# Fifteen small unread loads on ScalarE's DMA queue, in a decode-attention and SwiGLU kernel

## The chip, the cores and the metric

The kernel runs on one core of a Trainium2 chip. The metric is the time of one execution in microseconds (us), as the device measures it. A kernel's time is the median of its runs. "The profile" is one execution taken by the hardware profiler; its span is somewhat shorter than the measured time (136.8 us in the profile of the kernel before, against 138.75 us). "The trace" is what that profile was made from: each instruction, each semaphore update and each DMA packet with its start and length.

## The reference, cut to what matters

```python
h  = x + A(layernorm(x))      # A: q = x @ wq; attention over the last 2048 keys of k_cache and v_cache; @ wo
h2 = h + B(layernorm(h))      # B: (silu(h @ w1) * (h @ w3)) @ w2
# x is 4 x 1024, wq 1024 x 4096, k and v windows 4 x 4 x 2048 x 128, wo 4096 x 1024,
# w1 and w3 1024 x 3584, w2 3584 x 1024, all bf16
```

Four rows of x meet some 55 MB of weights and cache, so nearly all the work is loading.

## The kernel before: the parts that matter

All large loads go out on SyncE's queue, in one fixed order, into five buffers of 4 MB. x is loaded on ScalarE's queue.

```python
def load_rows(src, n, r0, pieces):
    t = stream.tile([P, SLOT], BF16, tag="s")              # 5 buffers
    i = 0
    for m in pieces:
        nc.sync.dma_start(
            out=t[:, i * n : (i + m) * n], in_=src[:, (r0 + i) * n : (r0 + i + m) * n]
        )
        i += m
    ...

# plan: wq in three loads (2 MB, 2 MB, 4 MB), k in four of 2 MB, v in four, wo, w1, w3, w2
x_sb = act.tile([B, D], BF16)
nc.scalar.dma_start(out=x_sb[:], in_=x_flat)
load_next(5)                                               # wq, k and half of v, as buffers allow
...
for j in range(JG):                                        # JG = 4
    nc.scalar.dma_start(
        out=x_q[QD * j : QD * (j + 1) : RS, :], in_=x_flat[:, j * CG : (j + 1) * CG]
    )
...
nc.scalar.activation(out=rstd[:], in_=mv[:, 1:2], func=ACT.Sqrt, ...)   # ScalarE's first activation
... # xn = layernorm(x), transposed; then the query matmuls q_ps, one group for each wq load
```

A completion semaphore is a counter that a DMA raises as it lands; whoever needs its data waits for the count. No semaphore is written in the source. The tile framework adds them when the program is built. In the built programs, the DMAs of SyncE's and ScalarE's queues together use **eight completion semaphores**, dealt out in turn in the order in which the framework schedules the DMAs. A DMA that is dealt a semaphore with an earlier holder is given a wait, on its issuing engine, for that holder's landing. This is the start of the deal before (numbers are semaphores 0 to 7):

```
x_sb 0, wq1 1, x_q 2 3 4 5, wq2 6, wq3 7          none of these waits for a holder
k1 waits for 0 (x_sb), k2 for 1 (wq1), k3 and k4 for 2 and 3 (x_q), v1 and v2 for 4 and 5, v3 for 6 (wq2), ...
```

## Time and profile before

| | before |
|---|---|
| time, median of 2 runs | 138.75 us (138.73 to 138.77) |
| span of the profile | 136.8 us |
| moved by DMA | 55.74 MB, mean 407 GB/s |
| busy: matrix engine, VectorE, ScalarE | 50%, 31%, 22% of the span |

From the page of the kernel before, the span in 40 equal slices of 3.42 us: the busy share of the 16 DMA engines in tenths, and what they moved.

```profile
DMA  5999999999999999999999999999999999998950
GB/s 156 441 418 503 402 393 441 421 431 436 421 431 421 436 436 417 433 445 469 450 421 402 407 427 441 453 441 402 427 449 453 411 419 424 450 460 364 418 219 2
```

The DMA engines never rest between the first slice and the last three. In the views below, L95 is line 95 of the kernel, PE is the matrix engine, DVE is VectorE and ACT is ScalarE; SPq and ACTq are instructions that issue DMAs on SyncE's and ScalarE's queues, and "issue" is time in which nothing was waited for. The chain of work that ended last (start, length, what) ends so:

```profile
95.26 0.42 SPq L95
95.69 0.04 issue
95.73 37.38 DMA t<-in_B_w_dram
133.11 0.04 issue
133.15 0.32 PE y_ps L430 x4
133.49 0.42 DVE res L440
```

The last load is issued at 95.7 us and lands 37.4 us later, because that much is queued ahead of it. The waits of the matrix engine for loads (total us, times, longest us):

```profile
PE q_ps L213 <- DMA t<-in_A_wq_dram: 11.9, 3, 7.8
PE u_ps L400 <- DMA t<-in_B_w_dram: 10.9, 2, 5.5
PE y_ps L430 <- DMA t<-in_B_w_dram: 8.1, 4, 6.5
PE g_ps L400 <- DMA t<-in_B_w_dram: 4.6, 1, 4.6
```

It waits at each stage of wq, w1, w3 and w2, so computing has slack there and the load stream has none. How the stream starts is in the timeline of SyncE's queue (start, length from the first to the last of the group, what):

```profile
0.73 1.47 SPq L95 DMA_DIRECT2D t<-in_A_wq_dram  x3
2.42 7.62 SPq L107 DMA_DIRECT2D t<-in_A_k_cache_dram  x4
```

and of ScalarE:

```profile
1.35 2.52 ACTq L146 DMA_DIRECT2D x_q<-in_A_x_dram  x4
3.90 1.28 ACT L160 ACT_TABLE_LOAD   x1 [3.90 <-DVE stats L156]
5.20 0.29 ACT L160 ACTIVATE rstd<-mv,eps_t 4x1 f32<-4x1 f32 x1
```

All three wq loads, 8.4 MB, are in the queue by 2.2 us.

### The profile page before, as it was taken

The page shows a single profiled execution, that of the slowest core. Times are in us where ns is not written, and L with a number is a line of the kernel's source. Part 1 is how long each engine was busy: PE and PEld are TensorE (multiplying, and loading weights), DVE is VectorE, ACT ScalarE, POOL GpSimd, SP SyncE. Part 2 cuts the span into 40 slices and gives each one's busy share as a digit, 9 for nine tenths or more (in the row PEclk, how much of TensorE's full clock was granted, in tenths as well). Part 3 has the DMA queues.
Part 4 walks back from the last instruction along what each step waited for, and adds up shares of the span by engine and source line. Part 5 has one row for each costly group of instructions (what it writes and reads, how often), then busy time and mean ns, then how long its engine had stood idle before and what let it go on. Part 6 is the DMA issues. An engine that isn't in the chain of part 4 may idle for free.

```text
span 136.8 us, 2307 instructions
## 1 busy us (share of the span) xinstructions
PE 68.3 (50%) x1035; PEld 42.3 (31%) x1035; DVE 43.0 (31%) x74; ACT 30.6 (22%) x35; POOL 1.7 (1%) x8
## 2 busy tenths in 40 slices
PE   0152303698989899105259259825080530802950
PEld 0110001274756565000149247602030210301820
DVE  6440000244444444709940030260004970170001
ACT  0400000155555646092943000000015000000000
POOL 5000000000000000000000000000000000000000
PEclk9999999999999999965555865896555586555586
DMA  5999999999999999999999999999999999998950
GB/s 156 441 418 503 402 393 441 421 431 436 421 431 421 436 436 417 433 445 469 450 421 402 407 427 441 453 441 402 427 449 453 411 419 424 450 460 364 418 219 2
DMA packets 3237, 55.74 MB, mean 407 GB/s; under 512 B 376, under 2 KB 408, under 8 KB 668
## 3 DMA queue, kind: packets, MB, share of 16 engines
q1 hardware_dynamic: 3188, 55.58, 95.2%
q8 instruction: 8, 0.13, 0.3%
q10 hardware_dynamic: 40, 0.02, 0.1%
q14 instruction: 1, 0.01, 0.0%
HBM read 55.59 MB, written 0.01 MB: 406 GB/s over the span
## 4 chain that ended last, share of the span: by engine, by line
DMA 43%; PE 29%; ACT 13%; DVE 8%; issue 4%; SPq 1%; ACTq 0%; DVEq 0%
DMA t<-in_B_w_dram 27%; DMA t<-in_A_wq_dram 15%; PE kt_ps L261 9%; ACT kT L267 6%; PE scores_ps L246 5%; PE OT_ps L324 5%; PE y_ps L351 4%; ACT z L302 3%; PE q_ps L213 2%; DVE rmax L278 2%; PE g_ps L400 2%; ACT Pm L283 2%; SPq L95 1%; DVE pT L292 1%; DVE z L298 1%
## 5 line engine op out<-in xcount | busy, mean ns | idle before, releaser
L267 ACT COPY kT<-kt_ps 128x1024 bf16<-128x1024 bf16 x16 | 15.8, 1014 | 12.0 <-PE kt_ps L261 12.0
L261 PE MATMUL kt_ps<-ident,t 128*128 128x128 bf16 x256 | 16.5, 220 | 0.0
L261 PEld LDWEIGHTS <-t 128*128 128x128 bf16 x256 | 14.4, 98 | 5.0 <-issue 4.9
L265 DVE COPY kT<-kt_ps 128x1024 bf16<-128x1024 bf16 x16 | 11.1, 692 | 15.2 <-PE kt_ps L261 15.2
L213 PE MATMUL q_ps<-t,xnT 128*4 128x512 bf16 x64 | 6.9, 596 | 11.9 <-DMA t<-in_A_wq_dram 11.9
L400 PEld LDWEIGHTS <-hnT 128*32 128x32 bf16 x128 | 4.9, 129 | 23.7 <-issue 20.8
L400 PE MATMUL u_ps<-t,hnT 128*32 128x448 bf16 x64 | 6.3, 573 | 10.9 <-DMA t<-in_B_w_dram 10.9
L246 PE MATMUL scores_ps<-kT,qz 128*32 128x512 bf16 x64 | 9.9, 609 | 3.1 <-ACT kT L267 2.9
L324 PE MATMUL OT_ps<-z,t 128*128 128x32 bf16 x256 | 7.5, 186 | 7.7 <-ACT z L302 5.0
L430 PE MATMUL y_ps<-t,hgT 128*32 128x256 bf16 x112 | 6.0, 384 | 8.1 <-DMA t<-in_B_w_dram 8.1
L324 PEld LDWEIGHTS <-t 128*128 128x128 bf16 x256 | 7.3, 102 | 8.4 <-issue 8.3
L400 PE MATMUL g_ps<-t,hnT 128*32 128x448 bf16 x64 | 5.2, 490 | 6.9 <-DMA t<-in_B_w_dram 4.6
L430 PEld LDWEIGHTS <-hgT 128*32 128x32 bf16 x112 | 4.6, 134 | 10.1 <-issue 5.8
L213 PEld LDWEIGHTS <-xnT 128*4 128x4 bf16 x64 | 2.0, 112 | 16.4 <-issue 16.0
L351 PE MATMUL y_ps<-t,o 128*32 128x256 bf16 x128 | 5.9, 372 | 0.8 <-DVE o L340 0.8
L223 DVE TENSOR_SCALAR q_sb<-q_ps 128x512 bf16<-128x512 f32 x1 | 0.7, 692 | 17.4 <-PE q_ps L213 17.4
L302 ACT ACTIVATE z<-pt_ps,mask 128x512 bf16<-128x512 f32 x8 | 5.3, 687 | 3.5 <-DVE z L298 3.5
L298 DVE TENSOR_SCALAR z<-pt_ps,mask 128x512 bf16<-128x512 f32 x8 | 5.5, 741 | 1.1 <-ACT z L302 0.8
L294 PE MATMUL pt_ps<-pT,perm 128*128 128x512 bf16 x4 | 2.4, 609 | 6.8 <-DVE pT L292 6.8
L414 DVE RECIPROCAL eg<-eg 128x896 f32<-128x896 f32 x1 | 5.8, 5752 | 0.0
L351 PEld LDWEIGHTS <-o 128*32 128x32 bf16 x128 | 4.4, 133 | 3.1 <-DVE o L340 1.9
L224 ACT ACTIVATE q_sb<-q_ps 128x512 bf16<-128x512 f32 x1 | 0.6, 597 | 21.1 <-DVE q_sb L223 21.1
(73 smaller groups left out, 40.3 us busy)
## 6 DMA issues: line engine op xcount, KB each, us to landing
t<-in_B_w_dram SPq DMA_DIRECT2D x4, 3584.0 KB
t<-in_A_k_cache_dram SPq DMA_DIRECT2D x4, 2048.0 KB, 25.4
t<-in_A_v_cache_dram SPq DMA_DIRECT2D x4, 2048.0 KB, 41.5
t<-in_A_wo_dram SPq DMA_DIRECT2D x2, 4096.0 KB, 42.2
t<-in_A_wq_dram SPq DMA_DIRECT2D x2, 2048.0 KB, 9.6
t<-in_A_wq_dram SPq DMA_DIRECT2D x1, 4096.0 KB, 21.0
t<-in_B_w_dram SPq DMA_DIRECT2D x1, 4096.0 KB, 37.7
t<-in_B_w_dram SPq DMA_DIRECT2D x1, 1280.0 KB, 34.4
```

The lines of the kernel that those rows point to most:

```text
L213: nc.tensor.matmul(q_ps[QD * g : QD * g + B, hf * 512 : (hf + 1) * 512], lhsT=xnT[:, kc, :], rhs=wq_t[:, c0 : c0 + 512], start=(kc == 0), ...
L246: nc.tensor.matmul(scores_ps[QD * g : QD * (g + 1), n * 512 : (n + 1) * 512], lhsT=qz[:, b, g * QD : (g + 1) * QD], rhs=kT_v[:, g, :, :], ...
L261: nc.tensor.transpose(out=kt_ps[:, jj, :], in_=k_v[:, n * NJ + t * TB + jj, :], identity=ident[:])
L265: nc.vector.tensor_copy(out=kT[:, t * TB : (t + 1) * TB, :], in_=kt_ps[:])
L267: nc.scalar.copy(out=kT[:, t * TB : (t + 1) * TB, :], in_=kt_ps[:])
L298: nc.vector.tensor_scalar(out=z[:, :, g, :], in0=pt_ps[:], scalar1=mask[:, g : g + 1], scalar2=None, op0=ALU.mult)
L302: nc.scalar.mul(out=z[:, :, g, :], in_=pt_ps[:], mul=mask[:, g : g + 1])
L324: nc.tensor.matmul(OT_ps[:, b, :], lhsT=loaded["v"][b][:, j, :], rhs=PTz[j // NJ][:, (j % NJ) * B + b, :, :], start=(j == 0), stop=(j == J ...
L351: nc.tensor.matmul(y_ps[QD * j : QD * (j + 1), :], lhsT=o4[:, i, :, :].rearrange("p b s -> p (b s)"), rhs=loaded["wo"][i][:, j * CG : (j + ...
L400: nc.tensor.matmul(out_ps[QD * j : QD * (j + 1), hf, :HF], lhsT=hnT[:, k, :], rhs=loaded[kind][k][:, c0 : c0 + HF], start=(k == 0), stop=( ...
L414: nc.vector.reciprocal(out=eg[:], in_=eg[:])
L430: nc.tensor.matmul(y2_ps[QD * j : QD * (j + 1), :], lhsT=hgT[:, i, :], rhs=loaded["w2"][i][:, j * CG : (j + 1) * CG], start=False, stop=(i ...
```

## The change

Fifteen small loads ("marks") of 1 to 15 rows of wq, each with its own row size of 32 to 256 bytes, follow the loads of x on ScalarE's queue. Nothing reads them, so the change can only show what such loads cost beside a full stream.

```diff
             out=x_q[QD * j : QD * (j + 1) : RS, :], in_=x_flat[:, j * CG : (j + 1) * CG]
         )
+
+    marks = wide.tile([16, 15, 128], BF16, tag="w4k")
+    for k in range(1, 16):
+        n = 8 + 8 * k
+        nc.scalar.dma_start(out=marks[0:k, k - 1, :n], in_=A_wq[0:k, 0:n])
```

The framework schedules eight marks ahead of the second wq load and the other seven ahead of the third. The deal in the built program of the changed kernel:

```
x_sb 0, wq1 1, x_q 2 3 4 5, marks 1 to 8: 6 7 0 1 2 3 4 5
wq2 6: waits for mark 1
marks 9 to 15: 7 0 1 2 3 4 5
wq3 6: waits for wq2
```

## The prediction

> What bounds the kernel now. It is bound by its stream of loads. The profile's slices show the DMA engines at 9 tenths in all but the first and the last few, at a mean of 407 GB/s. The chain of waits ends with 37.4 us of waiting for w2's last load, and the waits view shows the matrix engine idle for weights in every late stage (4.6, 5.5, 5.35 and 6.5 us). So computing has slack there, and the load stream has none: each microsecond in which SyncE's queue is empty should lengthen the run by about one.
>
> What the change adds. Under 20 KB. The x_q loads, of the same kind, take 0.63 us each to issue on ScalarE's queue (4 in 2.52 us, timeline), so 15 cost about 9.5 us of ScalarE before its first activation (now at 5.2 us). By itself that would hide: the query matmuls' last input lands at 22.6 us.
>
> What it moves is worse. The built programs show eight completion semaphores dealt out in turn to the DMAs of both queues; a DMA that gets a used one first waits for its former holder. Before, the three wq loads go out without a wait at 0.73 to 2.2 us. After, the second wq load waits for the first mark, and the third, which draws the same semaphore, waits for the second wq load's landing.
>
> First pause. The first mark stands in ScalarE's rings behind the four x_q loads. The Trainium skill, "DMA: Bandwidth & Descriptors", section "Queues, rings and completion order", says that each DMA engine takes turns between rings packet by packet. The trace agrees: x_q loads issued from 1.35 us move their first packets at 5.55 us only, and then a data and a completion packet each alternate with 0.61 us packets of wq. So the first mark cannot land before the first wq load has drained, at 7.2 to 7.7 us. I expect it at about 8.0. From issue to first packet the first wq load took 1.0 us, and its first packets 1.1 to 1.5 us against 0.61. Estimate: 2.2 us lost.
>
> Second pause. The second wq load would land at about 15 us (12.6 before); then landing, issue, first packet and ramp again. Estimate: 2.0 us lost. The third wq load lands at about 26.8 us instead of 22.6.
>
> ScalarE: marks 4 and 11 to 15 wait for the first wq load and for earlier marks; ScalarE is free at about 17 us, the query matmuls start at about 21 and the first half is done by 25, still before the third wq load. The k and v loads wait for marks too, but these land with over 10 us of loads still queued.
>
> Predicted: 138.75 + 4.2 = 143.0 us, range 141.4 to 145.2. Chances: faster by over 2% 0.01, within 2% 0.12, slower by over 2% 0.87.
>
> What would show it. The timeline of SyncE: second wq issue at about 8 us, third at about 15. Slices: GB/s low twice in the first 18 us, then as before. First activation at 17 to 19 us. The waits view: the last wait for wq ends at 26 to 27.5 us; w-stage waits unchanged.
>
> What would make it wrong. If the marks land while the first wq load still flows, the first pause shrinks. If marks on few rings land much later than estimated, k loads (which wait for marks 9 to 12) could open a third pause. If the later stream has hidden slack, less than 4 us shows.

## The result, and the profile after

| | before | after |
|---|---|---|
| time, median | 138.75 us (2 runs) | 144.3 us (143.84 and 144.75) |
| ratio, 95% interval | | 1.0398 (1.0362 to 1.0434): slower |
| span of the profile | 136.8 us | 142.9 us |
| moved by DMA | 55.74 MB | 55.77 MB |

The slices of the page after, 3.57 us each:

```profile
DMA  5939679999999999999999999999999999998950
GB/s 158 432 75 436 203 339 422 436 431 427 427 440 427 427 427 427 436 422 472 443 431 406 431 416 460 417 430 441 425 425 430 425 441 458 431 431 369 417 219 2
```

There are two holes, in the third slice and in the fifth and sixth. From the seventh on the rates are those of before. The timeline of SyncE's queue after, in short windows so that the three wq loads are not merged:

```profile
0.73 0.38 SPq L95 DMA_DIRECT2D t<-in_A_wq_dram  x1
8.66 0.33 SPq L95 DMA_DIRECT2D t<-in_A_wq_dram  x1
16.20 0.33 SPq L95 DMA_DIRECT2D t<-in_A_wq_dram  x1
16.57 2.73 SPq L107 DMA_DIRECT2D t<-in_A_k_cache_dram  x4
```

What SyncE's queue waited for (two lines that have no counterpart before):

```profile
SPq L95 <- DMA marks<-in_A_wq_dram: 7.5, 1, 7.5
SPq L95 <- DMA t<-in_A_wq_dram: 7.2, 1, 7.2
```

ScalarE, and the matrix engine's waits for loads:

```profile
3.90 12.46 ACTq L153 DMA_DIRECT2D marks<-in_A_wq_dram  x15
16.39 1.28 ACT L165 ACT_TABLE_LOAD   x1 [16.39 <-DMA marks<-in_A_wq_dram]
17.68 0.29 ACT L165 ACTIVATE rstd<-mv,eps_t 4x1 f32<-4x1 f32 x1
```

```profile
PE u_ps L405 <- DMA t<-in_B_w_dram: 10.7, 2, 5.4
PE y_ps L435 <- DMA t<-in_B_w_dram: 8.8, 4, 6.5
PE q_ps L218 <- DMA t<-in_A_wq_dram: 5.4, 1, 5.4
PE g_ps L405 <- DMA t<-in_B_w_dram: 4.2, 1, 4.2
```

The second wq load went out at 8.66 us, after 7.5 us of waiting for a mark, and the third at 16.20 us, after 7.2 us of waiting for the second. The waits for w1, w3 and w2 hardly changed.

The trace's DMA packets size the holes. No packet of SyncE's queue with data was moving on any engine for 2.06 us from 7.57 us and for 1.65 us from 15.52 us; before there is no such stretch of over 0.15 us. The completion packets of the second wq load begin at 12.03 us before and 15.05 after (3.0 us later), those of the third at 21.72 and 27.44 (5.7 us later), and the last 4 KB packets of the stream (those of the last load but one) end at 132.12 and 137.96 (5.8 us later). So the loss is made by 28 us and carried unchanged to the end. The packets also add up: from 4 to 32 us, averaged over the 16 engines, SyncE's queue moves no data for 4.7 us (3.7 us of it in the two full stops), and its large packets take 1.0 us longer than the usual 0.61 us per 16 KB and 1.21 us per 32 KB. Before, both sums are zero within 0.03 us. The profile is of the slower of the two runs, 144.75 us.

### The profile page after: what moved, and what is told of

Its sections match the earlier page's. It is cut to its first block, busy times and chain, and to the rows that moved or that the text cites. A ratio compares the mean times of both kernels' runs of the same rounds, so it can differ in the third digit from the quotient of the medians.

```text
span 142.9 us, 2324 instructions
## 1 busy us (share of the span) xinstructions
PE 69.5 (49%) x1035; PEld 43.1 (30%) x1035; DVE 43.0 (30%) x74; ACT 30.7 (21%) x35; POOL 1.7 (1%) x8
## 2 busy tenths in 40 slices
DMA packets 3478, 55.77 MB, mean 390 GB/s; under 512 B 616, under 2 KB 648, under 8 KB 908
## 4 chain that ended last, share of the span: by engine, by line
DMA 43%; PE 30%; ACT 11%; DVE 8%; issue 3%; ACTq 2%; SPq 1%; DVEq 0%
DMA t<-in_B_w_dram 26%; DMA t<-in_A_wq_dram 14%; PE kt_ps L266 10%; ACT kT L272 5%; PE scores_ps L251 5%; PE OT_ps L329 4%; PE y_ps L356 4%; DMA marks<-in_A_wq_dram 3%; ACT z L307 3%; PE q_ps L218 3%; PE g_ps L405 2%; ACTq L146 2%; DVE rmax L283 2%; ACT Pm L288 1%; DVE pT L297 1%
## 5 line engine op out<-in xcount | busy, mean ns | idle before, releaser
L266 PE MATMUL kt_ps<-ident,t 128*128 128x128 bf16 x256 | 17.5, 227 | 0.0
L266 PEld LDWEIGHTS <-t 128*128 128x128 bf16 x256 | 15.5, 102 | 4.9 <-issue 4.9
L405 PE MATMUL u_ps<-t,hnT 128*32 128x448 bf16 x64 | 6.3, 574 | 10.7 <-DMA t<-in_B_w_dram 10.7
L175 PE MATMUL tp_ps<-ident,xn 4*128 4x4 bf16 x8 | 0.7, 199 | 18.8 <-DVE xn L168 18.8
L329 PEld LDWEIGHTS <-t 128*128 128x128 bf16 x256 | 7.3, 103 | 7.4 <-issue 7.3
L405 PE MATMUL g_ps<-t,hnT 128*32 128x448 bf16 x64 | 6.3, 573 | 6.5 <-DMA t<-in_B_w_dram 4.2
L435 PEld LDWEIGHTS <-hgT 128*32 128x32 bf16 x112 | 4.3, 127 | 10.7 <-issue 6.4
L175 PEld LDWEIGHTS <-xn 4*128 4x128 bf16 x8 | 0.6, 163 | 18.8 <-DVE xn L168 18.8
L356 PE MATMUL y_ps<-t,o 128*32 128x256 bf16 x128 | 5.1, 329 | 0.8 <-DVE o L345 0.8
```

The costliest lines, as they stand in the source:

```text
L266: nc.tensor.transpose(out=kt_ps[:, jj, :], in_=k_v[:, n * NJ + t * TB + jj, :], identity=ident[:])
L329: nc.tensor.matmul(OT_ps[:, b, :], lhsT=loaded["v"][b][:, j, :], rhs=PTz[j // NJ][:, (j % NJ) * B + b, :, :], start=(j == 0), stop=(j == J ...
L356: nc.tensor.matmul(y_ps[QD * j : QD * (j + 1), :], lhsT=o4[:, i, :, :].rearrange("p b s -> p (b s)"), rhs=loaded["wo"][i][:, j * CG : (j + ...
L405: nc.tensor.matmul(out_ps[QD * j : QD * (j + 1), hf, :HF], lhsT=hnT[:, k, :], rhs=loaded[kind][k][:, c0 : c0 + HF], start=(k == 0), stop=( ...
L435: nc.tensor.matmul(y2_ps[QD * j : QD * (j + 1), :], lhsT=hgT[:, i, :], rhs=loaded["w2"][i][:, j * CG : (j + 1) * CG], start=False, stop=(i ...
```

## The experiments

Three theories:

- **A**: the marks take semaphores in the common deal, so that a wq load has to wait for a holder that lands late. The stream runs empty, and being the bound it hands the loss to the total.
- **B**: the marks hold up ScalarE (first activation at 17.68 instead of 5.20 us), and with it the query matmuls.
- **C**: many small packets slow the DMA engines themselves.

Twelve kernels ran, all correct, each in 3 rounds beside the kernel before, in three groups of four with one chip for each group (the kernel before took 138.83, 138.70 and 138.73 us there). "Loss" is a kernel's median less that of the kernel before in its group. "Idle" is the time within the stream in which no large data packet of SyncE's queue moves on any engine, and "end shift" how much later than 132.12 us the last 4 KB packet ends; both are from one profile each.

| kernel | time, us | ratio (95%) | loss | idle | end shift |
|---|---|---|---|---|---|
| n2, two marks | 138.64 | 0.9985 (0.997 to 1.0) | -0.2 | none | 0.0 |
| n3, three marks | 141.06 | 1.0159 (1.0141 to 1.0177) | 2.2 | 1.34 | 2.5 |
| n8, eight marks | 141.49 | 1.0197 (1.0176 to 1.0219) | 2.7 | 1.54 | 2.7 |
| chain, no marks, two waits | 143.52 | 1.0338 (1.0317 to 1.0359) | 4.7 | 1.38 + 1.27 | 5.2 |
| chain2, no marks, second wait | 141.19 | 1.0185 (1.017 to 1.02) | 2.5 | 1.27 | 2.4 |
| actbusy, no marks, ScalarE held | 138.62 | 0.9991 (0.9975 to 1.0008) | -0.1 | none | 0.1 |
| wqfirst, fifteen behind wq | 143.42 | 1.0338 (1.0322 to 1.0353) | 4.7 | 3.24 | 4.7 |
| sp, fifteen on SyncE's queue | 145.99 | 1.053 (1.0514 to 1.0545) | 7.3 | 4.91 | 7.1 |
| merged, one load | 138.89 | 1.0012 (0.9997 to 1.0026) | 0.2 | none | 0.1 |
| pool, fifteen on GpSimd's queue | 141.07 | 1.0166 (1.0148 to 1.0184) | 2.4 | none | 2.1 |
| pool1load, one load there | 138.81 | 1.0013 (0.9996 to 1.003) | 0.1 | none | 0.0 |
| pool1row, fifteen of one row there | 140.21 | 1.0112 (1.0097 to 1.0128) | 1.5 | none | 1.6 |

### How many marks: n2, n3, n8

```diff
-    for k in range(1, 16):
+    for k in range(1, 3):        # n2;  range(1, 4) in n3,  range(1, 9) in n8
```

The number of marks decides which semaphores the wq loads are dealt:

```
n2: wq2 waits for x_sb,   wq3 for wq1 (while wq2 still flows)
n3: wq2 waits for wq1,    wq3 for the first x_q load
n8: wq2 waits for mark 1, wq3 for mark 2 (which lands with it)
```

> Only the first two of the fifteen marks. Built program: the second wq load then waits for x_sb (landed at 2.5 us), the third wq load for the first wq load (landed at 8.2 us before), while the second wq load still has about 4 us to flow. Theory A (a load that waits for a semaphore's former holder empties the stream): no pause, 138.6 to 139.2 us. Theory B (each mark costs ScalarE issue time that delays the query matmuls): 2/15 of 5.5 us, so about 139.5 us. Theory C (small packets slow the DMA engines): also in proportion, under 139.5 us.

> One mark more than n2. Built program: now the second wq load waits for the landing of the first, and the third for an x_q load, so that it can follow at once. Theory A: exactly one pause, a step of 2.5 to 3.1 us over n2, 141.2 to 142.0 us, second wq issue at 8.2 us, third right behind it. Theories B and C: a step of about 0.4 us, 139.1 to 139.9 us.

> Eight marks. Built program: the second wq load waits for the first mark as in the changed kernel, but the third waits for the second mark, which lands with it. Theory A: one pause of about 3 us, 141.5 to 142.3 us, close to n3 although there are five more marks. Theories B and C: eight fifteenths of the loss, 141.7 us for 5.5 us, and clearly over n3 (by about 1.8 us). The pair n3 and n8 tells them apart.

SyncE's queue in n2, then in n3:

```profile
0.73 2.00 SPq L95 DMA_DIRECT2D t<-in_A_wq_dram  x2
8.21 0.33 SPq L95 DMA_DIRECT2D t<-in_A_wq_dram  x1
```

```profile
0.73 0.38 SPq L95 DMA_DIRECT2D t<-in_A_wq_dram  x1
8.04 0.81 SPq L95 DMA_DIRECT2D t<-in_A_wq_dram  x2
```

The third mark, three rows of 64 bytes, costs 2.4 us (141.06 less 138.64), and the next five cost 0.4 us together. In n2 a wq load also waits, until 8.21 us, but another 2 MB is in the queue meanwhile, and the wait is free. In n3 the queue is empty when the wait ends. That is the step of theory A; B and C, which go in proportion to the marks, fall as the cause of this step. It was a little under the 2.5 us expected, so that n3 came 0.1 us below its range, and n8 (141.49) missed its own by 0.01. Of the 0.4 us between n3 and n8, 0.3 go with the later end of the wait: the second wq load goes out at 8.32 us in n8 and 8.04 in n3.

### The waits without the marks: chain, chain2

```diff
+            d = nc.sync.dma_start(...)
+            if src is wq_v:
+                chain.append(d.ins)
+                if len(chain) > 1:                  # chain2: > 2
+                    tc.add_manual_dep(chain[-1], chain[-2].name, <wait for landing>)
```

> The kernel before, without any mark, but the second wq load made to wait for the landing of the first and the third for the landing of the second. Theory A: both pauses come without a mark, 143.6 to 144.6 us, second wq issue at 8.2 us, third at about 15.7. Theories B and C: no mark, no loss, 138.8 us.

> No marks; only the third wq load waits for the landing of the second, the second goes out at once. The second pause alone. From the runs so far (chain 143.5 less n3 141.1): 2.4 us, 140.9 to 141.4 us; third wq issue at 12.9 us, first k load landing 2.4 us later than before.

SyncE's queue in chain:

```profile
0.73 0.39 SPq L97 DMA_DIRECT2D t<-in_A_wq_dram  x1
8.19 0.33 SPq L97 DMA_DIRECT2D t<-in_A_wq_dram  x1
15.26 0.33 SPq L97 DMA_DIRECT2D t<-in_A_wq_dram  x1
```

With no mark in the program, the two waits alone cost 4.7 us of the 5.55. The waits are sufficient. The two add: the first pause alone costs 2.2 us (n3), the second alone 2.5 (chain2), and both together 4.7 (chain). chain came 0.1 us below its range. What remains to the changed kernel, about 0.9 us, goes with its longer holes: 2.06 + 1.65 us against 1.38 + 1.27. It is as large as the spread of the changed kernel's two runs, and so only roughly known.

### ScalarE held without marks: actbusy

```diff
+    junk = wide.tile([P, 2048], BF16, tag="w4k")
+    nc.gpsimd.memset(junk[:], 0.0)
+    junk2 = wide.tile([P, 2048], BF16, tag="w4k")
+    busy = [nc.scalar.copy(out=junk2[:], in_=junk[:]).ins for _ in range(6)]
-    nc.scalar.activation(out=rstd[:], in_=mv[:, 1:2], func=ACT.Sqrt, ...)
+    with tc.issue_after(busy[-1]):
+        nc.scalar.activation(out=rstd[:], in_=mv[:, 1:2], func=ACT.Sqrt, ...)
```

> No marks; six dummy copies of 128 x 2048 on ScalarE ahead of its first useful activation, which then comes at about 17 to 19 us, as in the changed kernel (17.7), instead of 5.2. Theory A: the query matmuls start late but the loads do not, 138.6 to 139.3 us. Theory B (ScalarE's delay is the cause): 143 us or more.

ScalarE in actbusy:

```profile
5.22 11.54 ACT L157 COPY junk<-junk 128x2048 bf16<-128x2048 bf16 x6
16.78 1.28 ACT L166 ACT_TABLE_LOAD   x1
18.07 0.29 ACT L166 ACTIVATE rstd<-mv,eps_t 4x1 f32<-4x1 f32 x1
```

The first activation is even later than in the changed kernel (18.07 against 17.68 us), and nothing is lost. Theory B falls.

### The pause moved: wqfirst, sp

In wqfirst the marks get an ordering edge, without a wait, to the third wq load, so that they are dealt their semaphores after it. In sp they are issued on SyncE's own queue, where the framework puts them after the first half of v.

```diff
 wqfirst:
-        nc.scalar.dma_start(out=marks[0:k, k - 1, :n], in_=A_wq[0:k, 0:n])
+        d = nc.scalar.dma_start(out=marks[0:k, k - 1, :n], in_=A_wq[0:k, 0:n])
+        tc.add_manual_dep(d.ins, chain[-1].name, <order only>)   # chain: the wq loads
 sp:
-        nc.scalar.dma_start(out=marks[0:k, k - 1, :n], in_=A_wq[0:k, 0:n])
+        nc.sync.dma_start(out=marks[0:k, k - 1, :n], in_=A_wq[0:k, 0:n])
```

> All fifteen marks on ScalarE's queue, but told to come behind the third wq load in the order in which the semaphores are dealt out. The wq loads then wait for nothing, but the first k load waits for the eighth mark, and that for the landing of the third wq load. Theory A: both early pauses are gone and one new one stands behind the third wq load, at about 22 to 25 us: one pause, 141.2 to 142.4 us; first wq inputs as before (22.6 us). Theories B and C: B 138.8 us (the first activation comes before the marks), C 144 us.

> All fifteen marks on SyncE's own queue, between the load of v's second part and its third. The wq and k loads wait for nothing new. Built program: the eighth mark waits for the landing of the second v load, which is the last load in the queue, and marks nine to fifteen are issued behind it before the next load of v. Theory A: one pause of about 4.4 us at 52 to 57 us (landing, eight issues of 0.3 us, first packet 1 us, slow first packets), 142.3 to 144.0 us, with all wq and k landings as before. Theories B and C: B 138.8 us (ScalarE is untouched); C a loss in proportion to the packets, which the deep queue should not change.

The chain of work in wqfirst, from its longest early wait on:

```profile
1.63 21.09 DMA t<-in_A_wq_dram
22.73 0.02 issue
22.75 1.28 DMA marks<-in_A_wq_dram
24.02 0.02 issue
24.04 7.93 DMA t<-in_A_k_cache_dram
```

The pauses at 7 and 15 us are gone and one stands where the deal says: mark 8 waits for wq3, and the first k load for mark 8. I had costed it as one pause of the usual size and missed the range (143.42 against 141.2 to 142.4): two landings stand in series, the second of 1.28 us, and the stream is idle for 3.24 us instead of 1.3 to 2.1. In sp the pause is far from the start. Busy time by stretch (start:end, length, then PE, weight loads, DVE, ACT and POOL, which is GpSimd, and PE's granted clock; the last two figures of a line are the DMA engines' busy share and GB/s):

```profile
30.00:52.40 22.40, 19.92 (x257) 13.30 (x256) 8.61 (x13) 12.95 (x14) 0.00 (x0) 1.00 0.95 403
52.40:57.40 5.00, 3.13 (x36) 1.53 (x33) 2.60 (x3) 2.02 (x2) 0.00 (x0) 1.00 0.07 20
57.40:132.00 74.60, 30.97 (x523) 19.45 (x524) 24.24 (x35) 12.68 (x16) 0.00 (x0) 0.57 1.00 427
```

Place and kind are as expected, 52.4 to 57.4 us at 20 GB/s; the size is not (7.3 us against 3.6 to 5.3). The idle time alone is 4.91 us where the whole pause was expected at 4.4, and the rest of the end shift, 2.2 us, is well over what a pause costs elsewhere beyond its idle time (below). The trace shows about 0.8 us of the difference: the second v load ends unevenly, so that from 51.5 to 52.45 us, before the stream is wholly empty, the DMA share is only 0.10.

### Fewer loads, and another queue: merged, pool, pool1load, pool1row

```diff
 merged (pool1load: nc.gpsimd):
-    for k in range(1, 16):
-        n = 8 + 8 * k
-        nc.scalar.dma_start(out=marks[0:k, k - 1, :n], in_=A_wq[0:k, 0:n])
+    nc.scalar.dma_start(out=marks[0:15, 14, :], in_=A_wq[0:15, 0:128])
 pool:
+        nc.gpsimd.dma_start(out=marks[0:k, k - 1, :n], in_=A_wq[0:k, 0:n])
 pool1row:
+        nc.gpsimd.dma_start(out=marks[0:1, k - 1, :n], in_=A_wq[0:1, 0:n])
```

> The fifteen rows of 256 bytes in one load on ScalarE's queue instead of fifteen loads. One semaphore drawn: the second wq load waits for nothing, the third for x_sb, landed at 2.5 us. Theory A: 138.6 to 139.2 us. Theory B: about 0.4 us over before. Theory C: the same number of the longest rows, so a part of the loss.

> All fifteen marks with the same bytes and rows, but issued on GpSimd's queue, whose loads draw from another set of semaphores; SyncE's and ScalarE's waits are those of the kernel before. Theory A: 138.6 to 139.3 us, the three wq issues between 0.7 and 2.3 us. Theory C (small packets in the DMA engines): most of the 5.5 us stays, over 142 us.

> To find why the marks on GpSimd's queue still cost 2.4 us though no wq load waited: the fifteen rows of 256 bytes as one load on GpSimd's queue. If the cost is per load (each ends in completion packets on all 16 engines): a fifteenth, 138.7 to 139.0 us. If any use of that queue costs: 141 us. If it is the rows: about 141 us.

> The counterpart: fifteen loads on GpSimd's queue, each of one row only. If the cost is per load: nearly the whole 2.4 us, 140.5 to 141.2 us. If it is per row: an eighth of it (15 of 120 rows), 139.0 us.

One load of fifteen rows of 256 bytes takes one semaphore and costs nothing that is clear of noise. The Trainium skill, "DMA: Bandwidth & Descriptors", section "Rules for kernel authors", advises to coalesce many small transfers because they are "mostly overhead". The advice holds here, for another reason: the overhead of two loads cost nothing either; what cost was which semaphore the next wq load got (n2 against n3).

pool was a miss. The fifteen marks draw from other semaphores, all three wq loads are issued between 0.74 and 2.07 us, the stream is never idle, and still 2.4 us are lost, on a queue that is not in the change. Two stretches of the kernel before, then of pool (last column GB/s):

```profile
12.00:30.00 18.00, 8.06 (x93) 3.97 (x92) 2.37 (x4) 1.93 (x3) 0.00 (x0) 1.00 1.01 435
30.00:132.00 102.00, 57.01 (x910) 36.83 (x907) 35.03 (x49) 27.10 (x31) 0.00 (x0) 0.72 1.00 427
```

```profile
12.00:30.00 18.00, 6.54 (x63) 2.25 (x62) 0.98 (x2) 0.60 (x1) 2.31 (x5) 1.00 0.98 396
30.00:132.00 102.00, 57.66 (x920) 38.06 (x921) 36.40 (x51) 28.44 (x32) 0.00 (x0) 0.74 1.00 430
```

The stream runs slower, 396 against 435 GB/s, while the DMA engines are hardly less busy (0.98 against 1.01): SyncE's own 16 KB packets take 0.67 us on average in this stretch, against 0.61 before. On GpSimd's queue a kind of theory C is right. The trace shows 480 packets there in pool and in pool1row, and 32 in pool1load: 32 for each load, whatever its rows. The number of loads makes 1.5 of the 2.4 us (pool1row, 0.3 us under its range); one load costs nothing clear of noise. The remaining 0.9 us goes with the rows, although the packets are no more. Why is open; no run here tells more.

On ScalarE's queue theory C has no such effect that shows. n2 and merged lose 0.2 us at most. In wqfirst 49 mark packets move beside the full stream by 22 us, and the third wq load ends 0.04 us later than before. In the changed kernel itself, about 100 of the 240 mark packets move in the two full stops and 94 more in the half microsecond in which the second wq load runs out. All 240 beside a full stream were not tried on that queue.

## Why the prediction was right, and where its terms were off

The measured 144.3 us lies inside the predicted 141.4 to 145.2, 1.3 us over the point. The mechanism held; both pauses were put too short.

- **"It is bound by its stream of loads ... each microsecond in which SyncE's queue is empty should lengthen the run by about one."** Right in kind, too small in size. In chain2 1.27 us idle shift the end by 2.4 us, in n3 1.34 by 2.5, in n8 1.54 by 2.7, in chain 2.65 by 5.2, in the changed kernel 3.71 by 5.8. Less the idle time that leaves 1.1 to 1.3 us for each pause.
- **The cause, the deal of semaphores.** Right, and shown from both sides: the waits without marks cost 4.7 us (chain), two marks that cause no harmful wait cost nothing (n2), and moving the marks in the deal moves the pause (wqfirst, sp).
- **"First pause ... I expect it at about 8.0"; "Estimate: 2.2 us lost".** The mechanism held: the first mark moved its data at 7.64 us, after the first wq load had run out at 7.57. The section cited, "Queues, rings and completion order", speaks of engines that take turns between rings by packets, and the trace after shows it again: x_q packets follow each other in steps of about 0.6 us while the first wq load flows (data at 5.47, completion at 6.10, data at 6.72 us), and in a burst from 7.3 us, when it ends. Why the first x_q packet moved only 4.1 us after its issue (1.34 us) is not told by the turns alone, and no run here shows it. The size was off: 3.0 us by the completion packets of the second wq load. The mark's semaphore was written only at 8.64 us, 1.0 us after its data; and the restart was mis-sized, as in the next point.
- **"Second pause ... Estimate: 2.0 us lost".** 2.7 us (5.72 less 3.02, from the completion packets). This is the term of the sum that was mis-sized: beyond the idle time, the prediction's only figure for the restart is that of the slow first packets. The first 16 packets of the second wq load do take 0.45 us longer each (1.06 against 0.61 us), but the engines also run out and start again one after another, over 0.5 us at the end (completion packets from 7.11 to 7.57 us) and 0.8 us at the start (first data packets from 9.63 to 10.39 us), and the whole comes to 1.1 to 1.3 us per pause. From issue to first packet it was 0.97 us at both pauses, as assumed. That is 0.64 us after the end of the issue instruction; the Trainium skill, same page, section "Latency and other measured facts", gives about 600 ns for a hardware queue's first byte. This trace agrees if one counts from the end of the issue instruction.
- **"15 cost about 9.5 us of ScalarE"; "free at about 17 us", "query matmuls start at about 21".** The marks took 0.25 to 0.44 us each to issue (4.9 us together), not the 0.63 of the x_q loads; 7.2 of the 12.46 us were four waits for semaphores. The sum was about right, for the wrong reason: free at 16.39, query matmuls at 19.71 us. That it would not matter is right, and actbusy shows it.
- **"w-stage waits unchanged"**: 4.2, 10.7 and 8.8 us against 4.6, 10.9 and 8.1. Right. "The last wait for wq ends at 26 to 27.5 us": 28.37, late for the same two terms.
- **"Under 20 KB."** The fifteen marks move 21.8 KB. Nothing rests on it.

## What to carry to other kernels

Look at the built program, not only at the source, before adding a DMA to a kernel that is bound by a stream: a load on another queue can take the completion semaphore that the stream's next load would have had, and the stream then waits for a stranger, or for its own last load. A wait is free while other loads are queued behind the same engines (n2) and costs its idle time and 1.1 to 1.4 us more in six kernels here (2.2 in sp) when the queue runs empty (n3). Put few, merged loads beside a stream, and see that the first two or three loads of the stream are issued without a wait.

## What the Trainium skill lacked or had wrong

- "DMA: Bandwidth & Descriptors", "Issuing engines are not separate DMA queues", says that DMAs of several engines interleave and that several issuers only save issue time. It lacks the tie that cost most here: the built programs deal eight completion semaphores to both hardware queues (the skill's start page, "Trainium Kernel Development and Optimization", "Key Constraints", counts 256 per core), and so loads on ScalarE's queue held SyncE's for 7.5 us, and through its own previous load for 7.2 us more.
- No page gives the cost of letting a full load stream run empty: idle time and 1.1 to 1.3 us beyond it in the changed kernel, n3, n8, chain and chain2; 1.4 us in wqfirst, 2.2 us in sp.
- "DMA: Bandwidth & Descriptors", "Rules for kernel authors": "mostly overhead" speaks of a transfer's own time; the page lacks what small loads can cost a stream beside them. The third mark cost 2.4 us, the next five 0.4 us together.
- The same page, "Why a DMA increments its semaphore by 16 and not by 1", tells that on GpSimd's queue all 16 engines post a completion whatever the shape, but not what it costs a running stream: 32 packets for each load here, and 1.5 us for fifteen loads of one row, 2.4 us for fifteen of 1 to 15 rows.
- The pages give a DMA's fixed cost as one rough figure; none tells how the time from a load's last data to its semaphore differs by load: the first mark's semaphore came 1.0 us after its 32 bytes had moved, the last increment of the first wq load 0.5 us after its last completion packet (7.66 and 8.19 us before).
